# A convolution and mixture kernel with two layer norms: second norm statistics from ScalarE squares and a ones column, base sums and tail in the common order, modulation weights streamed, phases as integers

## The chip, the cores and the metric

The kernel runs on one core of one Trainium2 chip. The metric is the time of one execution in device microseconds. Inputs and output are bfloat16 and lie in the chip's memory. The core's engines work through queues of their own, in order: TensorE (PE in the profile, with PEld for its weight loads), VectorE (DVE), ScalarE (ACT), GpSimd (POOL), and SyncE (SP), which here only issues transfers.

## The reference

One sequence of 2048 tokens and 640 channels. A vector c gives six rows of modulation; x is normed and modulated, a gated long convolution over the tokens is added to it, and it is normed again. A router then picks 8 tokens, which pass through a gated feed-forward layer and are added back.

```python
mod = (silu(c) @ w_mod)                      # sa, ca, ga, sb, cb, gb
h = layernorm(x) * (1 + ca) + sa
kv = shift_conv(k, shift_k) * v              # 4 taps over the tokens
y = irfft(rfft(kv, 4096) * rfft(ssm_k, 4096))[:2048] + kv * ssm_D
x = x + ga * (h * y)
h = layernorm(x) * (1 + cb) + sb
r = h @ w_r                                  # 8 best tokens
y = (silu(h_sel @ w_gate) * (h_sel @ w_up)) @ w_down * sigmoid(r_sel)
x = x + gb * (h + scatter(y))
```

## The kernel before

The 640 channels are cut into 5 blocks of 128 (b = 0 to 4), the 2048 tokens into 16 tiles of 128 (m). All of x stays on chip as `xq` [128 x 16 x 640]. The Fourier transform of length 4096 is done as matmuls in two stages, with tables made on the chip: `RA` and `RAT` (`short_tables`, L202) and `FT` (`t_TAB`, L233), with `IT` its transposes.

Each block b goes through a chain of tasks. `C` makes kv: 16 matmuls with diagonals `dg` of the taps, then VectorE multiplies by v, and the result goes to memory (`kvd`) and comes back in another layout (`xA`, LXA). `G` and `X` do the first stage for filter and kv (8 matmul groups, evacuated into `A`), `B` the second (evacuated into `HX`), `P` the complex product on VectorE (L324 to L328). `BT` transforms back and writes `U` to memory as `Ud` from GpSimd's queue, `LU` loads it again as `uA`, `AT` finishes the transform, multiplies by h and adds to `xq` (L380, L382). The evacuations from PSUM go to ScalarE, or to VectorE where the task's name carries a star (`Evac`, L46).

Beside the blocks stand `LW` and `MOD` (six slices of the modulation weights, of 640 columns each, loaded into six places, and ten matmuls for each), `OG` and `COL` (products of modulation rows, router column `wcol` and its sum `wsum`), `LX` (x into `xq`; three of the six weight slices use `xq` before it), `Sx` (first norm statistics), `H` (h, 12 steps on VectorE), `S` (second norm statistics, bn_stats on 80 pieces of 128 columns, L390), `R` (transposes of `xq` and small matmuls with `wcol`, summed into `rsum`), and `WG`, `WD` (feed-forward weights).

What sets the order is the table `ORDER` (L34): a list of task names, each advanced by the number of steps behind the colon. The engines' queues, SP's and GpSimd's among them, hold instructions in just this order. Buffers rotate in pools, and an instruction waits by semaphore for what it reads and for its buffer.

Behind the table (from L586) follows the tail in the order of the code: `moments` and `rsqrt` of the second norm, the router scores `r_bf`, `norm` (16 tiles, six of them on ScalarE), the top 8 by rank on small tiles, `base` (four matmuls of 320 columns a tile add x and sb*gb in PSUM, ScalarE copies the sum over `xq`, L621), the selection of the 8 tokens by a one-hot matmul (L688), gate, up and down projection (L700, L731), `finish` (two VectorE operations for two tiles, stores of four tiles, L704), and the scatter with addition of 8 rows from GpSimd's queue (L739). Base sums stand in four places between selection, gate, up and down; four of the eight pairs of `finish` stand behind the down projection's `delta`.

Of the kernel before, what the change touches and what calls it, by code (L numbers as in the profile page):

```python
# [9 lines left out]
P = 128  # L10
# [16 lines left out]
MAGIC = 1.5 * float(2 ** 23)  # L27
TWO_PI = 2 * math.pi
# [31 lines left out]
def _kernel_body(ctx, tc, A_q, A_k, A_v, A_shift_k, A_ssm_k, A_ssm_D,  # L60
# [15 lines left out]
    front = ExitStack()  # L76
    psum = front.enter_context(tc.tile_pool(name="psum", bufs=4, space=bass.MemoryType.PSUM))
# [38 lines left out]
    scr = early[:, 2560:2560 + 2560].bitcast(F32)  # L116
# [18 lines left out]
    mc64 = const.tile([P, 2], F32, name="mc64")  # L135
    pc = const.tile([P, 1], F32, name="pc")
# [11 lines left out]
    ang = scr[:, 0:512].rearrange("p (s n) -> p s n", s=4)  # L148
    qn = scr[:, 512:1024].rearrange("p (s n) -> p s n", s=4)
    a4 = scr[:, 1024:1152]  # L150
# [6 lines left out]
    def t_START():  # L157
        load_kv(0)
        with nc.allow_non_contiguous_dma(reason="tiny transposed loads"):
            nc.scalar.dma_start(out=shk_bf[:], in_=A_shift_k.rearrange("(b p) j -> p b j", p=P))  # L160
            load_g(0, nc.scalar)
            nc.scalar.dma_start(out=cT_bf[:], in_=c.rearrange("o (t p) -> p (o t)", p=P))
            nc.scalar.dma_start(out=wr_c[:], in_=B_w_r.rearrange("(t p) -> p t", p=P))
        iota(pidx[:], [[0, 1]], cm=1)
        iota(arow[:], [[1, M], [0, 8]])
        iota(erow[:], [[0, M], [1, 8]])
        make_identity(nc, ident[:])
        for hf in range(2):
            iota(trig[:, hf, :].rearrange("p (a b) -> p a b", a=8), [[4, 8], [64, P]], base=32 * hf + 1)
        nc.gpsimd.memset(halfpi[:], math.pi / 2)  # L170
        nc.gpsimd.memset(Dt[:], 0.0)
        iota(irow[:], [[1, P]])
        nc.gpsimd.memset(onesb[:], 1.0)
# [28 lines left out]
    def short_tables(s0):  # L202
        src, col = (a4, 0) if s0 == 0 else (arf, 1)
        sl = slice(s0, s0 + 2)
        for s, sh in ((s0, 0.25), (s0 + 1, 0.5)):
            V.tensor_scalar(out=ang[:, s, :], in0=src, scalar1=mc64[:, col:col + 1], scalar2=sh, op0=ALU.mult,
                            op1=ALU.add)
        V.tensor_scalar(out=qn[:, sl], in0=ang[:, sl], scalar1=MAGIC, scalar2=None, op0=ALU.add)
        V.tensor_scalar(out=qn[:, sl], in0=qn[:, sl], scalar1=-MAGIC, scalar2=None, op0=ALU.add)
        V.tensor_tensor(out=ang[:, sl], in0=ang[:, sl], in1=qn[:, sl], op=ALU.subtract)  # L210
        nc.scalar.activation(out=trg[:, sl], in_=ang[:, sl], func=ACT.Sin, scale=TWO_PI)
        if s0 == 0:
            V.tensor_scalar(out=msk[:, 0, :], in0=ef, scalar1=ecol[:], scalar2=None, op0=ALU.is_equal)
            yield
# [3 lines left out]
        else:  # L218
            V.tensor_scalar(out=msk[:, 1, :], in0=msk[:, 0, :], scalar1=1.0 / 2048, scalar2=None, op0=ALU.mult)
            yield  # L220
# [12 lines left out]
    def t_TAB(hf):  # L233

        k0 = 8 * hf
        ph, qq, ab = trig[:, hf, :], trig[:, 2, :], trig[:, 3, :]
        fl = lambda s: FT[:, s, k0:k0 + 8, :].rearrange("p a b -> p (a b)")
        V.tensor_scalar(out=qq, in0=ph, scalar1=pc[:], scalar2=MAGIC, op0=ALU.mult, op1=ALU.add)
        V.tensor_scalar(out=qq, in0=qq, scalar1=-MAGIC, scalar2=None, op0=ALU.add)
        yield  # L240
        V.scalar_tensor_tensor(out=ph, in0=ph, scalar=pc[:], in1=qq, op0=ALU.mult, op1=ALU.subtract)
        nc.scalar.activation(out=fl(1), in_=ph, func=ACT.Sin, scale=TWO_PI)
        yield
        nc.scalar.activation(out=ab, in_=ph, func=ACT.Abs)
        nc.scalar.activation(out=fl(2), in_=ph, func=ACT.Sin, scale=-TWO_PI)
        nc.scalar.activation(out=fl(0), in_=ab, func=ACT.Sin, scale=-TWO_PI, bias=halfpi[:])
        yield
# [113 lines left out]
    rsum = small.tile([P, M, 2], F32, name="rsum")  # L361
    wcol = const.tile([P, NB, 2], BF, name="wcol")
# [22 lines left out]
    def t_S(b):  # L385
        if b == 0:
            h_["st2"] = small.tile([P, M, NB, 6], F32, name="st2", tag="st")
        st2 = h_["st2"]
        for m in range(M):
            V.bn_stats(out=st2[:, m, b, :], in_=xq[:, m, b * P:(b + 1) * P])  # L390
            if m % 4 == 3:
                yield

    def t_R(b):
# [6 lines left out]
        pr = ps_tile([P, M, 2])  # L401
# [11 lines left out]
    def t_LW():  # L413
        xf = xq[:].rearrange("p m d -> p (m d)")
        spare = trig[:].rearrange("p s n -> p (s n)").bitcast(BF)
# [32 lines left out]
    def t_COL():  # L448
# [13 lines left out]
        V.tensor_tensor(out=wcol[:, :, 1], in0=wp[:], in1=wcol[:, :, 0], op=ALU.subtract)  # L462
        red = small.tile([P, 2], F32, name="red")
# [89 lines left out]
    def t_WD():  # L553
# [4 lines left out]
        yield  # L558


    tasks = {}

    def once(f, b):
        f(b)
# [234 lines left out]
```

## Time and profile before

| what | us |
|---|---|
| median of 3 runs | 213.3 (212.53 to 213.63) |
| profiled execution, its own time | 213.28 |
| its span | 211.5 |
| mean granted TensorE clock | 0.879 of full |

The span is what the profile covers, from the first to the last instruction. A timeline row has start, duration, engine, line, operation, output<-input, the number of instructions and in brackets the idle time ahead of it with what ended it. A row of a group has the count, then the busy time in all and the mean ns of one, then the idle time ahead of it. A row of a transfer has its count, size, and the median time from issue to landing. In the chain that ended last a row has start, duration and what ran. Lines are those of the kernel as printed above.

### The profile page before, as it was taken

To read this page: it belongs to the slowest core of one execution; us is meant where nothing else is said; L and a number is where in the kernel's file an instruction comes from. 1 tells how busy PE (TensorE), PEld (TensorE's weight loads), DVE (VectorE), ACT (ScalarE), POOL (GpSimd) and SP (SyncE) were. 2 spreads that over 40 slices of the span, in tenths; PEclk is the share of its full clock that TensorE was granted. 3 is DMA by queue.
4 is the path that set the end of the run, shared out by engine and by line. 5 is a ranking of instruction groups with operands and counts; after the bars stand their busy time and mean duration, and the time that the engine had idled before them with its cause. 6 is when DMAs were issued, how large, how long until landed. Compare 5 with 4: busy or idle time off the path is not lost.

```text
span 211.5 us, 3596 instructions
## 1 busy us (share of the span) xinstructions
PE 152.4 (72%) x1388; PEld 107.4 (51%) x1398; DVE 167.1 (79%) x368; ACT 131.8 (62%) x144; POOL 27.5 (13%) x59
## 2 busy tenths in 40 slices
PE   0659849997849998999978998675831069979600
PEld 0224627675627664757666776565720038644300
DVE  7769844696858999999999999999999891092930
ACT  0568745678857998999999998563221562520700
POOL 8843100000011300002001102110041000000002
PEclk9999997999699999999999999999785557575955
DMA  7999999999999939004979955677939000015060
GB/s 135 174 219 257 247 362 362 256 274 287 324 241 285 196 100 198 3 0 149 361 207 353 337 165 214 205 223 215 387 103 335 2 0 3 3 64 187 15 233 2
DMA packets 67897, 40.64 MB, mean 192 GB/s; under 512 B 44768, under 2 KB 64680, under 8 KB 67880
## 3 DMA queue, kind: packets, MB, share of 16 engines
q1 hardware_dynamic: 62376, 34.62, 60.7%
q0 software_dynamic: 1472, 5.25, 6.4%
q10 hardware_dynamic: 4032, 0.53, 1.9%
q8 instruction: 11, 0.18, 0.4%
q14 instruction: 6, 0.05, 0.1%
HBM read 24.67 MB, written 10.50 MB: 166 GB/s over the span
## 4 chain that ended last, share of the span: by engine, by line
DVE 47%; issue 23%; PE 15%; DMA 6%; ACT 3%; POOL 2%; POOLq 1%; SPq 1%; DVEq 0%
DVE st L390 6%; DMA vT<-in_A_v_dram 5%; DVE t L380 4%; DVE T L324 3%; PE py L731 3%; ACT HX L57 3%; DVE kvT L290 3%; DVE h L539 3%; DVE h L535 3%; DVE h L541 3%; DVE st L524 3%; PE ps L288 2%; DVE HX L325 2%; DVE xn L709 2%; DVE xn L708 2%
## 5 line engine op out<-in xcount | busy, mean ns | idle before, releaser
L57 ACT CAST A<-ps 128x1024 bf16<-128x1024 f32 x36 | 36.1, 1080 | 7.9 <-PE ps L267 7.8
L57 ACT CAST HX<-ps 128x1024 bf16<-128x1024 f32 x38 | 37.0, 1119 | 1.8 <-PE ps L310 1.8
L288 PE MATMUL ps<-kT,dg 128*128 128x512 bf16 x77 | 20.2, 403 | 10.9 <-DMA kT<-in_A_k_dram 7.1
L306 PE MATMUL ps<-A,FT 128*128 128x512 bf16 x73 | 27.7, 379 | 0.3 <-ACT A L57 0.3
L57 ACT CAST U<-ps 128x1024 bf16<-128x1024 f32 x20 | 19.6, 1075 | 4.4 <-issue 3.7
L308 PE MATMUL ps<-A,FT 128*128 128x256 bf16 x80 | 21.8, 272 | 0.4
L310 PE MATMUL ps<-A,FT 128*128 128x256 bf16 x80 | 21.8, 273 | 0.0
L340 PE MATMUL ps<-IT,HX 128*128 128x256 bf16 x80 | 19.0, 280 | 3.6 <-DVE HX L327 2.6
L346 POOL DMA_DIRECT2D Ud<-U x10 | 5.7, 568 | 107.7 <-ACT U L57 107.7
L629 ACT CAST xq<-po 128x640 bf16<-128x640 f32 x16 | 10.6, 693 | 14.5 <-PE po L628 12.8
L342 PE MATMUL ps<-IT,HX 128*128 128x256 bf16 x80 | 18.8, 280 | 1.0 <-DVE HX L328 1.0
L288 PEld LDWEIGHTS <-dg 128*128 128x128 bf16 x80 | 8.0, 102 | 20.5 <-DVE dg L229 7.0
L57 ACT COPY xT<-ps 128x2048 bf16<-128x2048 bf16 x5 | 9.3, 1870 | 12.8 <-PE ps L397 12.8
L290 DVE TENSOR_TENSOR kvT<-ps,vT 128x1024 bf16<-128x1024 f32 x10 | 12.0, 1220 | 6.7 <-PE ps L288 3.9
L390 DVE BATCH_NORM_STATS2 st<-xq 128x6 f32<-128x128 bf16 x80 | 16.1, 278 | 0.0
L375 PE MATMUL ps<-RAT,uA 128*128 128x128 bf16 x160 | 11.3, 228 | 3.9 <-DVE t L380 3.4
L267 PE MATMUL ps<-RA,gA 128*128 128x256 bf16 x80 | 11.0, 273 | 3.8 <-DVE gA L274 3.8
L324 DVE TENSOR_TENSOR T<-HX 128x2048 bf16<-128x2048 bf16 x10 | 12.2, 1222 | 1.3 <-ACT HX L57 0.7
L524 DVE BATCH_NORM_STATS2 st<-xq 128x6 f32<-128x320 bf16 x32 | 12.8, 477 | 0.0
L375 PEld LDWEIGHTS <-uA 128*128 128x128 bf16 x160 | 10.3, 103 | 4.6 <-DMA uA<-Ud 2.4
L310 PEld LDWEIGHTS <-FT 128*128 128x128 bf16 x80 | 7.8, 98 | 9.4
L325 DVE TENSOR_TENSOR HX<-HX 128x2048 bf16<-128x2048 bf16 x10 | 12.2, 1225 | 0.4
(198 smaller groups left out, 314.3 us busy)
## 6 DMA issues: line engine op xcount, KB each, us to landing
Ud<-U POOLq DMA_DIRECT2D x10, 512.0 KB, 5.1
uA<-Ud SPq DMA_DIRECT2D x10, 512.0 KB, 5.4
kvd<-kvT SPq DMA_DIRECT2D x5, 512.0 KB, 3.4
xA<-kvd SPq DMA_DIRECT2D x5, 512.0 KB, 5.4
xq<-in_A_q_dram SPq DMA_DIRECT2D x4, 640.0 KB, 7.0
out_dram<-xn SPq DMA_DIRECT2D x4, 640.0 KB, 3.2
xq<-in_w_mod_dram SPq DMA_DIRECT2D x3, 800.0 KB, 11.5
wg<-in_B_w_gate_dram SPq DMA_DIRECT2D x1, 2160.0 KB, 12.3
```

The lines of the kernel that those rows point to most:

```text
L57: self.nc.scalar.copy(out=out, in_=in_)
L288: nc.tensor.matmul(ps[:, i, :], lhsT=diags[b][:, j, :], rhs=kT[:, n0 - j:n0 - j + 512], start=(j == 0), stop=(j == 3))
L290: V.tensor_tensor(out=kvT[:, 1024 * i2:1024 * i2 + 1024], in0=ps[:].rearrange("p a b -> p (a b)"), in1=vT[:, 1024 * i2:1024 * i2 + 1024], ...
L306: nc.tensor.matmul(ps[:, i, :], lhsT=FT[:, 0, k2, :], rhs=f(A[:, 2 * k2:2 * k2 + 2]), start=True, stop=False)
L308: nc.tensor.matmul(ps[:, i, 0:256], lhsT=FT[:, 1, k2, :], rhs=f(A[:, 2 * k2 + 1:2 * k2 + 2]), start=False, stop=False)
L310: nc.tensor.matmul(ps[:, i, 256:512], lhsT=FT[:, 2, k2, :], rhs=f(A[:, 2 * k2:2 * k2 + 1]), start=False, stop=True)
L324: V.tensor_tensor(out=T2[:], in0=X, in1=Hi, op=ALU.mult)
L340: nc.tensor.matmul(ps[:, i, :], lhsT=hx[:, k2, 0, 1, :], rhs=IT[:, k2, 1:3, :].rearrange("p a b -> p (a b)"), start=True, stop=False)
L342: nc.tensor.matmul(ps[:, i, :], lhsT=hx[:, k2, 1, 1, :], rhs=IT[:, k2, 0:2, :].rearrange("p a b -> p (a b)"), start=False, stop=True)
L375: nc.tensor.matmul(o, lhsT=uA[:, bb, cs * P:(cs + 1) * P], rhs=RAT[:, cs, :].rearrange("p (m e) -> p m e", e=8), start=(cs == 0), stop=(cs ...
L390: V.bn_stats(out=st2[:, m, b, :], in_=xq[:, m, b * P:(b + 1) * P])
L524: V.bn_stats(out=st1[:, m, hf, :], in_=xq[:, m, hf * 320:hf * 320 + 320])
```

## The change

The arithmetic is regrouped and the order table is written anew; nothing of the computation is left out.

- **Second norm.** Instead of bn_stats, ScalarE squares `xq` and sums (16 times 512 columns for blocks 0 to 3, then 11 times 128 for block 4), VectorE does five of block 4's; the sum of x comes from a third column of ones in `wcol`.
- **Base sums** are made from `ident` and 512-column pieces ahead of the statistics, into buffers of their own, and 128-column rests (`BL`) in two steps. Norm outputs go to the places of `FT` and `IT`, results and stores use `xq`.
- **The tail** is cut into tasks `T`, `N`, `F`, `BS`, `BL` and stands in the same order table and the same PSUM pool.
- **Modulation weights** are streamed through two places of `early`; `LX` is cut into four steps.
- **Phases** are integers: GpSimd multiplies, VectorE masks, ScalarE's sine takes scale and bias.

```diff
 def t_START():
     load_kv(0)
+    load_g(0)
...
-        load_g(0, nc.scalar)
...
+        G.tensor_scalar(out=trig[:, hf, :].bitcast(I32), in0=trig[:, hf, :], scalar1=pidx[:], scalar2=None,
+                        op0=ALU.mult)
...
 def t_TAB(hf):
-    V.tensor_scalar(out=qq, in0=ph, scalar1=pc[:], scalar2=MAGIC, op0=ALU.mult, op1=ALU.add)
-    V.tensor_scalar(out=qq, in0=qq, scalar1=-MAGIC, scalar2=None, op0=ALU.add)
-    yield
-    V.scalar_tensor_tensor(out=ph, in0=ph, scalar=pc[:], in1=qq, op0=ALU.mult, op1=ALU.subtract)
+    V.tensor_scalar(out=ph, in0=ph, scalar1=8191, scalar2=None, op0=ALU.bitwise_and)
...
+def squares(b0, nb, ms, on_act):
+    dst = ssq[:, 0 if b0 == 0 else 1, :]
+    n = nb * P
+    for m in ms:
+        src = xq[:, m, b0 * P:b0 * P + n]
+        if on_act:
+            nc.scalar.activation(out=junk()[:, 0:n], in_=src, func=ACT.Square, accum_out=dst[:, m:m + 1])
+        else:
+            V.scalar_tensor_tensor(out=junk()[:, 1024:1024 + n], in0=src, scalar=1.0, in1=src, op0=ALU.mult,
+                                   op1=ALU.mult, accum_out=dst[:, m:m + 1])
...
+def t_BS():
+    for j in range(8):
...
+        for i in range(2):
+            nc.tensor.matmul(ps[:, i, :], lhsT=ident[:], rhs=gbs[:, 0:512], start=True, stop=False)
+            nc.tensor.matmul(ps[:, i, :], lhsT=ident[:], rhs=xq[:, 2 * j + i, 0:512], start=False, stop=True)
+        evac(h_["base", j // 4][:, 2 * j % 8:2 * j % 8 + 2, 0:512], ps[:])
+        yield
...
 def t_LW():
-    homes = [early[:, 2560:5760], early[:, 5760:8960], xf[:, 0:3200], xf[:, 3200:6400], xf[:, 6400:9600],
-             spare[:, 0:3200]]
     for a in range(6):
-        wms[a] = homes[a].rearrange("p (t d) -> p t d", t=NB)
+        wms[a] = early[:, a % 2 * 3200:a % 2 * 3200 + 3200].rearrange("p (t d) -> p t d", t=NB)
...
+def t_F():
+    for j in range(8):
+        x2 = xq[:, 2 * j:2 * j + 2, :]
+        V.tensor_tensor(out=x2, in0=xn(2 * j, 2).rearrange("p (m d) -> p m d", m=2),
+                        in1=gbo[:, None, :].to_broadcast([P, 2, D]), op=ALU.mult)
+        V.tensor_tensor(out=x2, in0=x2, in1=h_["base", j // 4][:, 2 * (j % 4):2 * (j % 4) + 2, :], op=ALU.add)
+        if j % 2 == 1:
+            nc.sync.dma_start(out=out_d[:, 2 * j - 2:2 * j + 2, :], in_=xq[:, 2 * j - 2:2 * j + 2, :])
+        yield
...
+    V.tensor_scalar(out=mu[:], in0=rsum[:, :, 2], scalar1=1.0 / D, scalar2=None, op0=ALU.mult)
+    V.tensor_tensor(out=msq[:], in0=mu[:], in1=mu[:], op=ALU.mult)
+    V.scalar_tensor_tensor(out=tot[:], in0=ssq[:, 0, :], scalar=D * EPS, in1=ssq[:, 1, :], op0=ALU.add, op1=ALU.add)
+    V.scalar_tensor_tensor(out=vv[:], in0=tot[:], scalar=1.0 / D, in1=msq[:], op0=ALU.mult, op1=ALU.subtract)
```

The last line of the new table, with `BS*` and the like for an evacuation on VectorE:

```diff
+BS* S LU4 BS* R2 R3* WG S:2 AT4:2 SV TC R3 R4* SA:2 WD BS* BS R4 T BS:4 N* BL N:3 N*:2 N T F N T N* N N*:3 T
+F:2 N:3 T BL F:3 T:2 F:2 T:3
```

How the queues change shows at three places. First SP's queue near the start, before (kvd_196 and kvd_250 are blocks 0 and 1, early, xq and trig the places of the weight slices):

```order
L295 DMA kvd_196<-kvT 128x2048
L95 DMA_TRANSPOSE kT<-in_A_k_dram 128x2048
L96 DMA_TRANSPOSE vT<-in_A_v_dram 128x2048
L295 DMA kvd_250<-kvT 128x2048
L111 DMA xA<-kvd_196 128x16x128
L420 DMA early<-in_w_mod_dram 128x5x640 x2
L420 DMA xq<-in_w_mod_dram 128x5x640 x2
L295 DMA kvd_358<-kvT 128x2048
L106 DMA gA<-in_A_ssm_k_dram 128x16x128
```

and the same place in the change, where kvd_200 and kvd_263 are blocks 0 and 1:

```order
L297 DMA kvd_200<-kvT 128x2048
L106 DMA gA<-in_A_ssm_k_dram 128x16x128
L111 DMA xA<-kvd_200 128x16x128
L297 DMA kvd_263<-kvT 128x2048
L563 DMA xq<-in_A_q_dram 128x4x640
L111 DMA xA<-kvd_263 128x16x128
L95 DMA_TRANSPOSE kT<-in_A_k_dram 128x2048
L96 DMA_TRANSPOSE vT<-in_A_v_dram 128x2048
L563 DMA xq<-in_A_q_dram 128x4x640
L466 DMA early<-in_w_mod_dram 128x5x640
```

xA of block 0 has moved ahead of block 2's k and v; the first weight slice has moved behind both xA and half of x, and three more slices follow only after block 4's k and v.

Second, ScalarE's queue from the last transposes on, before (rs_1967 is the second norm's factor, po the base sums):

```order
L57 COPY xT<-ps 128x2048 x5
L616 ACTIVATE xn<-xq,nm_1986,rs_1967 128x640 x6
L629 CAST xq<-po 128x640 x4
L716 ACTIVATE gs<-pm 128x112
L629 CAST xq<-po 128x640 x4
L722 ACTIVATE sig_2328<-inf 8x1
L629 CAST xq<-po 128x640 x8
```

and in the change (FT and IT hold the norm outputs, rs_113 is the factor):

```order
L58 COPY xT<-ps 128x2048
L400 ACTIVATE junk,ssq<-xq 128x512 x16
L400 ACTIVATE junk,ssq<-xq 128x128 x11
L58 CAST base<-ps 128x2x512 x5
L58 CAST base<-ps 128x8x128
L621 ACTIVATE FT<-xq,nm_114,rs_113 128x640 x5
L621 ACTIVATE IT<-xq,nm_114,rs_113 128x640 x4
L58 CAST base<-ps 128x8x128
L725 ACTIVATE gs<-ps 128x112
L733 ACTIVATE sig_2295<-inf 8x1
```

27 squares have come in, nine norms instead of six, and seven base evacuations stand ahead of gs instead of ones on both sides of it.

Third, VectorE's queue from the middle of block 4's last update on, before:

```order
L380 TENSOR_TENSOR t<-ps,h 128x1024
L382 TENSOR_TENSOR xq<-xq,t 128x16x64
L407 TENSOR_TENSOR rsum<-rsum,ps 128x32
L390 BN_STATS st_1301<-xq 128x6 x24
L407 TENSOR_TENSOR rsum<-rsum,ps 128x32
L485 TENSOR_REDUCE bs<-st_1301 128x16
```

and in the change:

```order
L383 TENSOR_TENSOR t<-ps,h 128x1024
L385 TENSOR_TENSOR xq<-xq,t 128x16x64
L402 SCALAR_TENSOR_TENSOR junk,ssq<-xq 128x128 x5
L457 TENSOR_TENSOR rsum<-rsum,ps 128x48
L56 COPY xT<-ps 128x2048
L56 CAST base<-ps 128x2x512
L457 TENSOR_TENSOR rsum<-rsum,ps 128x48
L639 TENSOR_SCALAR mu<-rsum 128x16
```

The 24 statistics have become five squares, and one transpose copy and one base evacuation have come between the last update and the second norm's first operation.

More of the change, by code (lines that the diff above doesn't have):

```diff
@@ L27 @@
 MAGIC = 1.5 * float(2 ** 23)
+PI = 3.1415925
 TWO_PI = 2 * math.pi
@@ L621, in base @@
-    def base(ms):
-        for m in ms:
-            po = back.tile([P, 2, 512], F32, name="po", tag="o", bufs=2)
-            for hf in range(2):
-                cc = slice(hf * 320, hf * 320 + 320)
-                nc.tensor.matmul(po[:, hf, 0:320], lhsT=ident[:], rhs=gbs[:, cc], start=True, stop=False)
-                nc.tensor.matmul(po[:, hf, 0:320], lhsT=ident[:], rhs=xq[:, m, cc], start=False, stop=True)
-            nc.scalar.copy(out=xq[:, m, :].rearrange("p (h d) -> p h d", h=2), in_=po[:, :, 0:320])
@@ L678, in _kernel_body @@
-    V.tensor_copy(out=cinfo[:, 1:3], in_=cvp[:])
-    norm(rest[4:])
-    base(range(0, 4))
-    pin = pm_tile([NSEL, 3])
-    nc.tensor.matmul(pin[:, :], lhsT=ohC[:], rhs=cinfo[:], start=True, stop=True)
-    xsT = small.tile([P, NB, NSEL], BF, name="xsT")
-    pxs = pm_tile([P, NB, NSEL])
-    for b in range(NB):
-        for m in range(M):
-            nc.tensor.matmul(pxs[:, b, :], lhsT=xn[m // 8][:, m % 8, b * P:(b + 1) * P], rhs=onehot[:, m, :],
-                             start=(m == 0), stop=(m == M - 1))
```

417 lines of the change are left out of this document (217 added, 200 removed).

## The prediction

> **What bounds the kernel now.** I read the page's totals first, then busy time in four stretches, then the timelines of the engines and the chain that ended last. The first row is the page's; the others have start and end of a stretch, its length, the busy time of each engine (PE is TensorE, DVE VectorE, ACT ScalarE, POOL GpSimd), granted clock, DMA share and GB/s.
>
> ```profile
> PE 152.4 (72%) x1388; PEld 107.4 (51%) x1398; DVE 167.1 (79%) x368; ACT 131.8 (62%) x144; POOL 27.5 (13%) x59
> ...
> 0.00:62.00 62.00, 44.22 (x298) 28.83 (x302) 46.01 (x90) 39.08 (x42) 13.97 (x32) 0.94 1.06 262
> 62.00:134.40 72.40, 64.74 (x501) 46.48 (x507) 68.34 (x116) 65.65 (x71) 7.58 (x16) 1.00 0.69 194
> 134.40:156.30 21.90, 15.01 (x239) 13.78 (x239) 21.66 (x63) 9.30 (x6) 1.54 (x3) 0.92 0.74 246
> 188.60:195.60 7.00, 6.97 (x30) 3.37 (x30) 3.14 (x5) 0.00 (x0) 0.00 (x0) 0.57 0.54 190
> ```
>
> VectorE is the busiest engine and is idle 16.0 of the first 62 us, while the DMA share stands at 1. From 62 to 156.3 it works 90.0 of 94.3, with ScalarE close beside it until 134.4 and more than half free after. Call 134.4, the end of the last product P4, **T**, and 156.3, the end of the last add of the convolution's result into xq, **X**. From X on there is a serial tail of 55.2 us:
>
> ```profile
> 133.76 0.68 DVE L328 TENSOR_TENSOR HX<-HX,T 128x1024 bf16<-128x1024 bf16 x1
> ...
> 156.30 4.73 DVE L390 BATCH_NORM_STATS2 st<-xq 128x6 f32<-128x128 bf16 x24
> ...
> 161.07 0.36 DVE L485 TENSOR_REDUCE bs<-st 128x16 f32<-128x160 f32 x1
> ...
> 163.48 0.17 DVE L499 TENSOR_SCALAR n2v<-bw 128x16 f32<-128x16 f32 x1
> ...
> 166.72 0.23 DVE L605 TENSOR_SCALAR r_bf<-r,wsum 128x16 bf16<-128x16 f32 x1
> ...
> 172.14 2.23 DVE L618 TENSOR_SCALAR xn<-xq,rs,nm 128x640 bf16<-128x640 bf16 x6
> ...
> 177.67 0.20 DVE L694 TENSOR_TENSOR xsT<-xsf,mc 128x40 bf16<-128x40 f32 x1
> ...
> 188.63 6.88 PE L731 MATMUL py<-wd,hT 128*8 128x320 bf16 x28 [1.56 <-DVE hT L726]
> ...
> 196.36 0.80 DVE L708 TENSOR_TENSOR xn<-xn,modv 128x1280 bf16<-128x1280 bf16 x1
> ...
> 203.12 3.21 DMA out_dram<-xn
> ```
>
> So the tail reads: statistics 4.8 (to 161.07), moments and rsqrt 5.9 (to r_bf at 166.95), top-k, norms and selection 10.9 (to xsT at 177.87), gate and up with base sums between them 10.8, down projection 6.9, and 16.0 after it, in which four output pairs (6.8, 1.69 each) and the last store (landed at 206.33) still stand ahead of the scatter.
>
> **Part 1, up to T: VectorE's work.** Each half of the phase tables loses three passes and gets one integer mask. A dozen small START and short-table passes go to GpSimd or vanish. Twelve of 80 statistics ahead of T go. Twelve evacuations instead of 7 stand ahead of T, and one more update (t, then xq).
>
> ```profile
> L238 DVE TENSOR_SCALAR trig<-trig,pc 128x1024 f32<-128x1024 f32 x2 | 1.5, 744 | 0.0
> ...
> L241 DVE SCALAR_TENSOR_TENSOR trig<-trig,pc 128x1024 f32<-128x1024 f32 x2 | 2.7, 1339 | 0.0
> ...
> L55 DVE CAST A<-ps 128x1024 bf16<-128x1024 f32 x4 | 4.8, 1218 | 4.2 <-PE ps L267 4.2
> ...
> L380 DVE TENSOR_TENSOR t<-ps,h 128x1024 bf16<-128x1024 f32 x10 | 12.1, 1214 | 0.0
> ...
> L382 DVE TENSOR_TENSOR xq<-xq,t 128x1024 bf16<-128x1024 bf16 x10 | 6.9, 692 | 0.3
> ```
>
> The three passes are two like L238 and L241: 2.8 a half, 5.6. An integer mask is not in the trace; between 0.74 and 1.34 I take L238's: two cost 1.5, so 4.1 are saved. Small passes: about 3 (estimate, 12 at 0.15 to 0.4). Statistics: 12 at 0.2 (24 took 4.73), 2.4. Against this 5 x 1.22 = 6.1 and 1.9 for the update. Net some 1.4 saved.
>
> **Part 1: VectorE's idle time.** The waits that matter, and their prices:
>
> ```profile
> 30.48 2.56 PE L432 MATMUL ps<-early 128*128 128x320 bf16 x10 [2.99 <-DMA early<-in_w_mod_dram]
> ...
> 33.93 2.36 DVE L55 CAST A<-ps 128x1024 bf16<-128x1024 f32 x2 [4.18 <-PE ps L267]
> ...
> 2.12 2.11 POOL L155 IOTA trig<- 128x1024 f32 x2
> ...
> 5.75 4.22 POOL L229 TENSOR_SCALAR dg<-ident,shk_f 128x128 bf16<-128x128 bf16 x4 [0.79 <-DVE shk_f L226]
> ...
> L198 POOL TENSOR_SCALAR tri<-irow,pidx 128x128 bf16<-128x128 f32 x1 | 0.6, 627 | 0.0
> ...
> L193 POOL TENSOR_SCALAR mC<-pidx 128x1 f32<-128x1 f32 x1 | 0.2, 183 | 0.0
> ...
> kvd<-kvT SPq DMA_DIRECT2D x5, 512.0 KB, 3.4
> xA<-kvd SPq DMA_DIRECT2D x5, 512.0 KB, 5.4
> ...
> xq<-in_w_mod_dram SPq DMA_DIRECT2D x3, 800.0 KB, 11.5
> ...
> early<-in_w_mod_dram SPq DMA_DIRECT2D x2, 800.0 KB, 8.2
> ```
>
> Now stage X0 stands on TensorE behind the first modulation matmul, which waits for its weights; the new order puts it ahead. kvd0 can leave near 15.5 (below), land in 3.4, xA0 in another 5.4: X0 near 25 instead of 33. The 4.2 us wait goes, and with it about 2 behind it. **What is late next**: the first quarter of q, whose statistics move up to this place (I charge 2), and GpSimd, which now makes the phases. Its 1024-wide multiply is not in the trace. From 0.18 for one column and 0.63 for 128, that is 3.5 ns a column, it is 3.7; its ends are the 1.05 of an iota as wide and 8 x 1.06 = 8.4, from four dg that took 4.22 beside a busy VectorE. I take 3.7, nearest to the plain fp32 row. With the first iota done near 5 the second phase table is ready near 13.5; its mask (0.75) stands on VectorE ahead of the second kvT (1.2), hence 15.5; I charge 1. So 3 us less idle; ends: 6 less (neither charge) to 6 more (multiplies at 8.4, twice 4.7, less the 3). T = 134.4 - 1.4 - 3 = 130.0.
>
> The Trainium skill, GPSIMD Engine Reference, Performance versus the Vector engine, speaks against this move: GpSimd is about half as fast as VectorE at elementwise work and needs about 2.6 cycles an element at 1.2 GHz. That would be an estimated 2.2 us a multiply, and T 1 us earlier; the 3.5 ns a column of the trace is dearer than the page's figure.
>
> **Part 2, T to X.** Now 21.9, all VectorE: 7 updates (13.3) and 44 statistics (8.7). After: 6 updates (11.4), two xT and two base evacuations (4.9), small ones (0.4): 16.7. But uA4's path becomes late. Its last evacuations now end 3.1 after T, at 137.45; then write, load, matmul:
>
> ```profile
> 135.52 1.93 ACT L57 CAST U<-ps 128x1024 bf16<-128x1024 f32 x2 [2.64 <-issue]
> ...
> Ud<-U POOLq DMA_DIRECT2D x10, 512.0 KB, 5.1
> uA<-Ud SPq DMA_DIRECT2D x10, 512.0 KB, 5.4
> ```
>
> 3.1 + 5.1 + 5.4, about 1.2 for two issues and 0.9 for sixteen matmuls are 15.7, where VectorE arrives at 12.9. Two updates (3.8) follow: X = 130.0 + 19.5 = 149.5.
>
> **Part 3, the tail.** ScalarE squares 16 rows of 512 columns from the last AT3 update on (some 12 before X), then 11 of 128 after X.
>
> ```profile
> L211 ACT ACTIVATE early<-early 128x256 bf16<-128x256 f32 x2 | 0.8, 416 | 1.2 <-DVE early L210 1.1
> ...
> 166.07 4.98 ACT L616 ACTIVATE xn<-xq,nm,rs 128x640 bf16<-128x640 bf16 x6 [6.55 <-DVE nm L600]
> ...
> 118.81 7.43 ACT L57 CAST HX<-ps 128x1024 bf16<-128x1024 f32 x8
> ...
> L688 PE MATMUL pm<-onehot,xn 128*128 128x8 bf16 x80 | 2.2, 166 | 0.0
> ...
> L700 PE MATMUL pm<-xsT,wg 128*128 128x8 bf16 x70 | 2.0, 168 | 0.5 <-DVE xsT L694 0.5
> ```
>
> A square with a sum is not in the trace. A wide one lies between 0.42 (256 columns) and 0.93 (1024, from 7.43 for 8); I take 0.75, nearest to the 0.83 of 640. A narrow one: 0.15 to 0.42, I take 0.35. The wide ones then end at X, the narrow at X+4; at the upper ends X+3 and X+8. Beside them block 4's row sums need transposes, a copy behind five VectorE squares, and 16 small matmuls behind eight base matmuls at half clock: about X+5.4. The chain starts at X+5.5, now 4.8: no gain. It has 18 small operations; now 17 lie between 163.48 and 166.72: 3.7 to r_bf, at X+9.2.
>
> The Trainium skill, ScalarE: Activation LUTs, What ACT_TABLE_LOAD costs, gives 186 ns and 0.833 a column, 93 for each pointer operand, 93 overlapped. That is 0.81 for the 640-column norm, and the 0.83 here agrees; a wide square would be an estimated 0.52 and end 3.7 earlier. The page has no price for the sum, and X+5.4 would still hold.
>
> Selection needs all 16 normalized tiles. ScalarE first has six base evacuations (0.93 each), until about X+10.5, then nine norms (0.83): X+18; 80 matmuls add 2.2. VectorE has three norms fewer than now in this place (7.4 falls to 6.3), but three output pairs (5.1), and some 2 of waiting for a transpose queued on TensorE behind cold base matmuls: 13.5, xsT at X+22.7. Here the change loses 2.6. But gate and up run back to back, 2.0 each, with three pairs beside them: 5.2 to the down projection instead of 10.8. It takes 6.9 again. Behind it stand only delta (0.9) and the scatter, 5.2 from its release to the end (206.33 to 211.5): 6.1 instead of 16.0, since all eight pairs are ahead. 5.5 + 3.7 + 13.5 + 5.2 + 6.9 + 6.1 = 40.9, against 55.2.
>
> 149.5 + 40.9 = 190.4 of span. The profiled execution took 213.28 for its 211.5, so 1.8 lie around it, and the median of three runs is 213.3. Forecast **192.2 us**.
>
> **Rivals.**
> 1. GpSimd contended: multiplies at 8.4 delay the front by 6 to 9: 198 to 202. The 4.22 of dg speaks for it; against it, VectorE has less to do there than now.
> 2. ScalarE overfull: the chain starts at X+8 to X+10 and the norms follow: 195 to 198.
> 3. A warm TensorE: 6.9 x 0.57 is 3.9 at full clock, so 189; with the front's lower end 184. The Trainium skill, TensorE: Matmul & The Clock Gate, Part 1, gives full clock after about 3.4 us of sustained work; the mean of 0.57 over seven dense microseconds here does not bear that out.
> 4. **Slower: the streaming.** Six weight slices share two buffers. Slice a waits for matmul a-2; SP, in order, holds k, v and g loads behind it, and TensorE everything behind a modulation matmul. Five landings laid bare at 8.2 to 11.5 are 41 and more: 233. It decides from 4.2 us exposed per slice, 21 in all. Against it: counting VectorE's work ahead of each place in the new order and 12 of idle, the second and third go out near 49 for use near 58 to 62, and the last is needed only ahead of h, near 88.
> 5. It doesn't do what it says: the statistics change engine and X to chain start stays as long. That I expect (5.5 against 4.8); the gain rests on the order of pairs, gate and up, which the queues fix.
>
> **How the numbers follow.** Forecast (187 to 196) 0.55; rival 1 0.13; rival 2 0.12; rival 3 0.11; rival 4 in part (203 to 212) 0.03 and whole 0.06. The range 184 to 202 takes in the ends of T and of the squares. A measurement of this kernel tells 0.5% (1.1 us) from no change: faster 0.91, same 0.02, slower 0.07.
>
> **What would show it.** X0 near 25 and no TensorE wait over 3 us on a modulation slice: streaming is hidden. T near 130, X near 150, narrow squares done near X+4, gate and up without base sums between them, nothing but delta and the scatter behind py. Wrong: T at 134 or later means that the new order brought nothing, and a delta that waits for pairs that the end is no shorter.

## The result, and the profile after

| | before | after |
|---|---|---|
| median | 212.9 us (212.53 to 213.63, 4 runs) | 189.3 us (188.03 to 190.83, 4 runs) |
| profiled execution, its span | 213.28, 211.5 | 188.81, 187.0 |

The ratio is 0.889 (95% interval 0.882 to 0.897): 11% faster, where 192.2 us was forecast. The first view is the busy time by stretch, cut at the same events as before: T, X, r_bf, xsT, start and end of py.

```profile
0.00:62.00 62.00, 49.82 (x340) 32.05 (x341) 50.95 (x82) 44.67 (x47) 24.98 (x48) 0.97 1.02 239
62.00:130.20 68.20, 62.31 (x533) 46.26 (x531) 63.44 (x106) 58.20 (x63) 4.44 (x10) 0.97 0.82 237
130.20:146.20 16.00, 11.89 (x190) 10.00 (x187) 15.76 (x20) 11.93 (x26) 6.00 (x12) 1.00 0.80 264
146.20:157.70 11.50, 9.38 (x60) 4.96 (x60) 7.24 (x32) 11.03 (x36) 0.83 (x3) 0.85 0.72 238
157.70:169.70 12.00, 3.94 (x88) 2.99 (x89) 10.96 (x35) 9.57 (x12) 0.00 (x0) 0.59 0.11 40
169.70:175.10 5.40, 4.97 (x144) 4.14 (x143) 5.06 (x10) 1.36 (x3) 0.00 (x0) 0.50 0.46 157
175.10:181.70 6.60, 6.54 (x28) 3.13 (x28) 3.19 (x6) 0.00 (x0) 0.00 (x0) 0.60 0.59 202
```

The columns are those of the same view of the kernel before. Up to T VectorE works as long as before: 50.95 + 63.44 = 114.4, against 46.01 + 68.34 = 114.35. Its idle time fell from 20.05 to 15.8. From T to X it works 15.76 of 16.0, where it worked 21.66 of 21.9. The timelines of the engines, at the events:

```profile
129.56 0.68 DVE L330 TENSOR_TENSOR HX<-HX,T 128x1024 bf16<-128x1024 bf16 x1
...
145.47 0.69 DVE L385 TENSOR_TENSOR xq<-xq,t 128x1024 bf16<-128x1024 bf16 x1
...
151.53 0.18 DVE L640 TENSOR_TENSOR msq<-mu 128x16 f32<-128x16 f32 x1
154.55 0.17 DVE L641 SCALAR_TENSOR_TENSOR tot<-ssq 128x16 f32<-128x16 f32 x1 [2.85 <-ACT junk L400]
...
157.42 0.23 DVE L648 TENSOR_SCALAR r_bf<-r,wsum 128x16 bf16<-128x16 f32 x1
...
169.49 0.20 DVE L710 TENSOR_TENSOR xsT<-xsf,mc 128x40 bf16<-128x40 f32 x1
...
175.09 6.54 PE L738 MATMUL ps<-wd,hT 128*8 128x320 bf16 x28 [0.43 <-DVE hT L729]
...
181.68 0.87 DVE L743 SCALAR_TENSOR_TENSOR delta<-ps,sig,modv 8x640 bf16<-8x640 f32 x1 [3.34 <-PE ps L738]
182.88 1.51 POOL L747 DMA_INDIRECT out_dram<-delta,idx  x1 [27.15 <-DVE delta L743]
```

The mean is ready at 151.5, and VectorE waits 2.85 for ScalarE's squares: a new wait at the head of the serial chain. Gate and up have no base sums between them, and nothing but delta and the scatter stands behind py. The tail from X to the end is 40.8, against 55.2.

### The profile page after: what moved, and what is told of

Its sections match the earlier page's. It is cut to its first block, busy times and chain, and to the rows that moved or that the text cites. A ratio compares the mean times of both kernels' runs of the same rounds, so it can differ in the third digit from the quotient of the medians.

```text
span 187.0 us, 3521 instructions
## 1 busy us (share of the span) xinstructions
PE 148.8 (80%) x1374; PEld 103.5 (55%) x1374; DVE 157.4 (84%) x283; ACT 136.8 (73%) x184; POOL 37.8 (20%) x74
## 4 chain that ended last, share of the span: by engine, by line
DVE 32%; ACT 20%; PE 20%; DMA 12%; issue 6%; POOL 6%; POOLq 1%; SPq 0%; DVEq 0%
ACT junk L400 8%; DVE t L383 5%; PE ps L290 5%; ACT HX L58 3%; DMA early<-in_w_mod_dram 3%; DMA xq<-in_A_q_dram 3%; POOL trig L178 3%; DVE kvT L292 3%; DVE h L586 3%; PE ps L478 3%; DVE h L584 3%; DVE h L580 3%; ACT base L58 3%; DMA uA<-Ud 3%; DVE T L326 3%
## 5 line engine op out<-in xcount | busy, mean ns | idle before, releaser
L58 ACT CAST A<-ps 128x1024 bf16<-128x1024 f32 x34 | 33.4, 1059 | 6.9 <-PE ps L269 6.9
L58 ACT CAST HX<-ps 128x1024 bf16<-128x1024 f32 x36 | 35.4, 1060 | 3.6 <-PE ps L312 3.4
L308 PE MATMUL ps<-A,FT 128*128 128x512 bf16 x80 | 30.5, 382 | 1.4 <-ACT HX L58 0.6
L310 PE MATMUL ps<-A,FT 128*128 128x256 bf16 x80 | 21.9, 274 | 0.0
L312 PE MATMUL ps<-A,FT 128*128 128x256 bf16 x80 | 21.9, 273 | 0.0
L58 ACT CAST U<-ps 128x1024 bf16<-128x1024 f32 x19 | 18.5, 1087 | 2.9 <-issue 1.5
L342 PE MATMUL ps<-IT,HX 128*128 128x256 bf16 x80 | 18.1, 272 | 0.3 <-DVE t L383 0.3
L344 PE MATMUL ps<-IT,HX 128*128 128x256 bf16 x80 | 18.1, 272 | 0.0
L400 ACT ACTIVATE junk<-xq 128x512 bf16<-128x512 bf16 (+1 forms) x27 | 13.5, 499 | 2.6 <-DVE xq L385 1.7
L478 PE MATMUL ps<-early 128*128 128x320 bf16 x60 | 10.3, 328 | 2.8 <-DVE early L473 2.0
L269 PE MATMUL ps<-RA,xA 128*128 128x256 bf16 x80 | 12.1, 298 | 0.1
L383 DVE TENSOR_TENSOR t<-ps,h 128x1024 bf16<-128x1024 f32 x10 | 12.2, 1216 | 0.0
L233 POOL TENSOR_SCALAR dg<-ident,shk_f 128x128 bf16<-128x128 bf16 x16 | 11.7, 746 | 2.1 <-PE ps L290 2.1
```

The costliest lines, as they stand in the source:

```text
L58: self.nc.scalar.copy(out=out, in_=in_)
L269: nc.tensor.matmul(ps[:, bb // 2, :, (bb % 2) * 8:(bb % 2) * 8 + 8], lhsT=src[:, 4 * g4 + bb, :], rhs=RA[:].rearrange("p k c e -> p (k c) ...
L308: nc.tensor.matmul(ps[:, i, :], lhsT=FT[:, 0, k2, :], rhs=f(A[:, 2 * k2:2 * k2 + 2]), start=True, stop=False)
L310: nc.tensor.matmul(ps[:, i, 0:256], lhsT=FT[:, 1, k2, :], rhs=f(A[:, 2 * k2 + 1:2 * k2 + 2]), start=False, stop=False)
L312: nc.tensor.matmul(ps[:, i, 256:512], lhsT=FT[:, 2, k2, :], rhs=f(A[:, 2 * k2:2 * k2 + 1]), start=False, stop=True)
L342: nc.tensor.matmul(ps[:, i, :], lhsT=hx[:, k2, 0, 1, :], rhs=IT[:, k2, 1:3, :].rearrange("p a b -> p (a b)"), start=True, stop=False)
```

## Experiments

The theory: T to X is VectorE's own work, so the statistics count whole; the order of the pairs saves what stood behind py; the front gained because X0 no longer waits for a modulation product; the squares on ScalarE cost some 3 at the chain's start. Ratios are to the kernel before on the same chip, with 95% intervals. The yardstick is the changed kernel run again:

> The changed kernel as it is, on the same chip as the next three: the yardstick for differences of a few us, since two profiles with the same front showed T at 130.2 and at 132.2. Expected 188 to 191.

189.0 us, ratio 0.895 (0.890 to 0.900), T at 131.0. In six other kernels whose code up to T is the change's, profiles have T between 129.1 and 132.2, so one profile tells T to about 1.5. The intervals of the next two kernels are some 0.02 to either side, which is 4 us.

### Statistics back on VectorE

```diff
-AT2:2 BT4:2 LU3 AT3 R1 AT3 S R1 R2*
-BS* S LU4 BS* R2 R3* WG S:2 AT4:2 SV TC R3 R4* SA:2 WD BS* BS R4 T
+AT2:2 BT4:2 LU3 AT3 R1 AT3 S0:4 R1 R2* S1:4
+BS* LU4 BS* R2 R3* WG S2:4 S3:4 AT4:2 TC R3 S4:4 R4* WD BS* BS R4 T
```

`S` is bn_stats as in the kernel before, and `moments` takes the place of the new sums.

> The changed kernel with only the second norm's statistics put back to bn_stats on VectorE: 64 pieces between the updates of block 3 and of block 4, 16 behind the last update and ahead of the transposes' copy; ScalarE's 27 squares and VectorE's five are gone. Theory A (VectorE's work sets T to X, so statistics taken off it are worth their whole time): X moves from 146.2 by 64 x 0.197 = 12.6 to about 158.8, r_bf by about 13 with the longer moments, of which some 1.5 come back because ScalarE's base sums are done ahead of the norms: 188.8 + 11 = about 200. Theory B (the gain is all in the order of the tail, and the squares cost at the chain's start what they save before X): within 2 us of 189.

Ratio 0.945 (0.926 to 0.963), 199.7 us: some 10.6 more than the changed kernel (0.050 of 212). Last add, first operation of the moments, and r_bf on VectorE's timeline:

```profile
157.17 0.69 DVE L385 TENSOR_TENSOR xq<-xq,t 128x1024 bf16<-128x1024 bf16 x1
...
163.37 0.36 DVE L536 TENSOR_REDUCE bs<-st 128x16 f32<-128x160 f32 x1
...
168.25 0.23 DVE L649 TENSOR_SCALAR r_bf<-r,wsum 128x16 bf16<-128x16 f32 x1
```

T is at 129.6, so T to X is 28.3 instead of 15.9: the 64 pieces add 12.4, nearly the 12.6 expected as their whole time. The moments start 5.5 after X instead of 8.4, and r_bf is 10.8 later; from there it is 28.2 to the end instead of 29.6, of which 1.0 is a shorter py. Theory A holds.

### Last four pairs behind delta

```diff
-F:2 N:3 T BL F:3 T:2 F:2 T:3
+F:2 N:3 T BL F T:4 F:4 T
```

> The changed kernel with only the last four output pairs moved behind delta, as they stood before. Theory A (what stands between delta and the scatter is laid bare whole): four pairs of 1.65 are 6.6, then a store that lands 3.2 after its issue, ahead of the scatter: about 199, py end to span end about 15.5 instead of 5.4. Theory B (the pairs only fill time that VectorE waits anyway, and the scatter does not wait for them): under 2 us.

Ratio 0.940 (0.922 to 0.959), 200.3 us, some 9.6 more. From the chain that ended last, and GpSimd's timeline:

```profile
189.78 0.84 DVE xq L631
190.64 3.21 DMA out_dram<-xq
...
194.91 1.51 POOL L747 DMA_INDIRECT out_dram<-delta,idx  x1 [37.24 <-issue]
```

delta ended at 184.2; the scatter started 10.7 later, behind four pairs and a store, and from py's end to the end of the span it is 15.7 (15.5 expected). Theory A holds.

### The pairs alone, and with the base sums ahead, in the kernel before

```diff
-    finish(range(2, 4))
+    finish(range(2, 8))
     delta = ...
-    finish(range(4, 8))
```

and in the second kernel also `base(range(8, 16))` ahead of py instead of 8 to 10 there and 10 to 16 behind it.

> The kernel before with one part of the change alone: the last four output pairs moved ahead of delta. Theory A (the order of the pairs works only together with the early base sums): pair 4 runs beside py, but pairs 5 to 7 wait for base sums that stand behind py on TensorE; the last store lands about 1 earlier than at 206.3: 0.5 to 2 less than before. Theory B (the order of the pairs by itself brings what it costs to undo it in the changed kernel): 7 to 10 less.

> The kernel before with two parts of the change: the last four pairs ahead of delta, and the last six base sums ahead of py on TensorE instead of behind it. Theory A (pairs and base sums go together): py starts some 4 later for 24 more matmuls and ScalarE's copies, but the pairs end beside it and nothing but delta and the scatter stands behind: 3 to 5 less than before, against 1.8 less for the pairs alone. Theory B (what matters is that the base sums leave the tail altogether): what the pairs gain the later py takes back, 0 to 2 less than before.

Ratios 0.990 (0.986 to 0.994) and 0.993 (0.989 to 0.997): 2.1 and 1.5 us less than before. py of the first and its last store; then py of the second, and on its VectorE the first operation after xsT and delta:

```profile
189.10 3.97 PE L731 MATMUL py<-wd,hT 128*8 128x320 bf16 x28 [1.57 <-DVE hT L726]
...
199.27 3.22 DMA out_dram<-xn
```

```profile
193.27 3.97 PE L731 MATMUL py<-wd,hT 128*8 128x320 bf16 x28
...
186.78 0.14 DVE L723 TENSOR_SCALAR sig<-sig 8x1 f32<-8x1 f32 x1 [6.52 <-ACT sig L722]
...
200.06 0.87 DVE L735 SCALAR_TENSOR_TENSOR delta<-py,sig,modv 8x640 bf16<-8x640 f32 x1
```

In the first, delta has to wait for the pairs, and one of these 0.4 for a base sum behind py; the store ends at 202.5 and the scatter begins at 203.5. In the second, py starts 4.2 later, but that is not what holds the end: py is over at 197.2, and delta starts at 200.1, straight behind the pairs and without a wait. In both kernels VectorE idles 6.5 us while gate and up run, and six pairs, 10 us, then stand between hT and delta. For the second kernel the time is theory B's, though not for the reason that B gives.

So undoing the pair order costs 9.6, but doing it alone, or with base sums still in the tail, brings 2. In the change three pairs run ahead of xsT and three more beside gate and up, and they can because their base sums are made by then. That this is what makes the difference is read from the traces; no run moved the base sums alone. Nor do all of them stand ahead of the statistics: of the eight sums of 512 columns VectorE copies two at 138.9 and one at 149.8, and ScalarE copies five from 154.4 on, behind its squares and ahead of its norms.

### The first modulation product ahead of X0

```diff
-... C0 LG1 G0*:3 G0 RAT DIAG1 LXA0 C1:2 IT:2 G1* IT* X0 X0* X0 X0*
+... C0 LG1 LW G0*:3 G0 RAT DIAG1 LXA0 C1:2 IT:2 G1* IT* RAT MOD X0 X0* X0 X0*
```

> The changed kernel with the first modulation slice loaded and multiplied ahead of stage X0, as it stood before; streaming and all else stay. Theory A (X0 ahead of the modulation product is what the front gained): X0 starts 3 to 5 us later than 23.5, T goes from 130.2 to about 133, time about 192. Theory B (VectorE's 11 us of idle time in the front absorb it): T within 1 us, time 188 to 190.

Ratio 0.906 (0.887 to 0.925), T at 130.7. The time does not separate the theories; T is within the changed kernel's 129.1 to 132.2, though X0 starts at 28.5 instead of 23.5. Here the weights are asked for so early that they have landed; the product waits 3.5 for a copy on VectorE instead. The next kernel asks for them behind xA0 (`... LXA0 C1:2 LW IT:2 ...`):

> As the kernel with the first modulation slice ahead of stage X0, but its weights are asked for only behind xA0 in SP's queue, so that the product waits for its transfer and holds X0 as it did before. Theory A (the exposed wait was what the front lost): MOD waits some 5 to 7 for its weights, X0 starts near 31 to 33 as before, T goes from about 131 to 134 to 135, time 192 to 193. Theory B (VectorE meets its later waits earlier and nothing is lost): X0 as late, but T within 1.5 of the changed kernel's 130.2 and 131.0.

Ratio 0.915 (0.908 to 0.921): some 4 us more than the changed kernel, outside both intervals. TensorE, then VectorE's last product:

```profile
30.23 2.54 PE L478 MATMUL ps<-early 128*128 128x320 bf16 x10 [4.35 <-DMA early<-in_w_mod_dram]
32.56 2.60 PE L269 MATMUL ps<-RA,xA 128*128 128x256 bf16 x16
```

```profile
136.84 0.68 DVE L330 TENSOR_TENSOR HX<-HX,T 128x1024 bf16<-128x1024 bf16 x1
```

X0 starts at 32.6, as it did before (32.8), and T moves to 137.5, which is 5 to 8 later than the changed kernel's 129.1 to 132.2. This one execution took 1.3 us more than its median, and its first filter stage was slow ahead of the edit (3.59 instead of 1.92, see below), so the 4 us of the times are the better measure. The transfer laid bare ahead of X0 costs these 4 us, as theory A says; X0 5 us late behind a product whose weights lie ready moves T by less than the scatter. Whether it is the transfer itself or what it delays in SP's queue was not separated.

### Phases in floating point again

```diff
-        V.tensor_scalar(out=ph, in0=ph, scalar1=8191, scalar2=None, op0=ALU.bitwise_and)
+        V.tensor_scalar(out=qq, in0=ph, scalar1=pc8[:], scalar2=MAGIC, op0=ALU.mult, op1=ALU.add)
+        V.tensor_scalar(out=qq, in0=qq, scalar1=-MAGIC, scalar2=None, op0=ALU.add)
+        V.scalar_tensor_tensor(out=ph, in0=ph, scalar=pc8[:], in1=qq, op0=ALU.mult, op1=ALU.subtract)
```

> The changed kernel with the long tables' phases in floating point again: GpSimd's two multiplies go, VectorE makes three passes a half instead of one mask. Theory A (VectorE's wait of 1.42 for GpSimd gives back most of the 3.8 of work that was saved): second kvT ends about 1 us later, time about 190. Theory B (the work saved counts whole): 193. Theory C (GpSimd was the brake): 187 to 188.

Ratio 0.907 (0.892 to 0.922), 192.1 us, T at 133.5: some 2.6 more, nearer to B, though the interval reaches A and no change at all. The first filter stage on TensorE, in this kernel and in the changed one:

```profile
15.88 3.48 PE L272 MATMUL ps<-RA,gA 128*128 128x256 bf16 x16 [4.99 <-DVE gA L279]
```

```profile
14.56 1.92 PE L269 MATMUL ps<-RA,gA 128*128 128x256 bf16 x16 [3.07 <-DVE gA L276]
```

VectorE reaches it 1.3 later, which is the phases' own doing. That the sixteen matmuls take 3.48 instead of 1.92 is not: in the changed kernel's second run they took 3.46 too, behind a wait of only 2.14. Of nine executions with the change's code up to there, three took 1.92, one 2.43 and five 3.46 to 3.59, behind waits of 2.1 to 3.7 in no order. T lies at 129.1 to 130.2 in the three and at 130.5 to 132.2 in the others that keep the change's code up to T. Against those, the 133.5 here is 1.3 to 3.0 later.

### A warm TensorE

```diff
+    def warm(n):
+        pw = ps_tile([P, 512])
+        for _ in range(n):
+            nc.tensor.matmul(pw[:, :], lhsT=ident[:], rhs=gbs[:, 0:512], start=True, stop=True)
```

`warm(5)`, `warm(7)` and `warm(4)` stand in the three waits of the selection.

> The changed kernel with 16 matmuls of 512 columns added whose results nobody reads, in three places of the tail where TensorE waits for VectorE (5 behind the scores' transpose, 7 behind the candidates' products, 4 behind the one-hot product). Theory A (idling in the selection is what lowers the granted clock): the clock stays above 0.9 until py, py falls from 6.5 towards 3.9 and gate and up from 3.9 towards 3. Then the last pair's store, at present landing 1.1 ahead of delta's end, holds the scatter, so the time falls by 1 to 2 only. Theory B (gate, up and the selection's 8-column matmuls do not hold the clock): the clock is near 0.5 again in gate and up, py stays at 5.5 to 6.5 and the time within 1 of the kernel without them.

Ratio 0.896 (0.889 to 0.902): no change. Stretches of this kernel, then the same of the changed kernel's second run (the third number from the end is the granted clock):

```profile
165.00:169.70 4.70, 3.37 (x85) 2.50 (x84) 4.62 (x10) 2.96 (x4) 0.00 (x0) 0.85 0.14 48
169.70:175.00 5.30, 5.30 (x145) 4.20 (x142) 4.86 (x9) 1.36 (x3) 0.00 (x0) 0.50 0.60 207
```

```profile
165.00:169.70 4.70, 2.54 (x76) 2.22 (x76) 4.63 (x10) 3.06 (x4) 0.00 (x0) 0.50 0.12 41
169.70:175.10 5.40, 5.40 (x148) 4.30 (x146) 4.92 (x10) 1.36 (x3) 0.00 (x0) 0.50 0.60 206
```

The clock rose from 0.50 to 0.85 in the one-hot stage, and fell to 0.50 again in gate and up; py took 5.31, against 5.27 without. Theory B holds, and rival 3 can't be had this way.

### The chain's start, and the tail's order

The first kernel moves six narrow squares to VectorE (`SV` in steps of 5, 2 and 4 rows, `SA` one of 5) and the row sums ahead of two base sums:

```diff
-R4* SA:2 WD BS* BS R4 T
+R4* SA WD SV R4 SV BS:2 T
```

> The changed kernel with six of block 4's eleven ScalarE squares moved to VectorE (two behind the last transposes' copy, four behind its row sums), the row sums ahead of two base sums, and the evacuation of one base sum moved from VectorE to ScalarE. Theory A (the squares on ScalarE hold the chain's start, and ScalarE's queue of base sums and norms holds the selection): VectorE's sum of squares starts near X+5.9 instead of X+8.4, r_bf near X+8.8 instead of X+11.4, but xsT only about 1.3 earlier, since ScalarE still has seven base sums and nine norms ahead of it: about 1.3 less. Theory B (r_bf alone holds the selection): all 2.5 arrive, 2.5 less. Theory C (the row sums hold the start, not the squares): no gain.

```profile
150.77 0.17 DVE L643 SCALAR_TENSOR_TENSOR tot<-ssq 128x16 f32<-128x16 f32 x1 [0.47 <-ACT junk L400]
...
156.87 0.28 DVE L659 CAST rT<-ps 16x128 f32<-16x128 bf16 x1 [1.73 <-PE ps L657]
...
165.27 0.19 PE L707 MATMUL ps<-onehot,IT 128*128 128x8 bf16 x1 [0.62 <-ACT IT L623]
```

and the last of these in the changed kernel:

```profile
167.32 0.19 PE L705 MATMUL ps<-onehot,IT 128*128 128x8 bf16 x1 [0.62 <-ACT IT L621]
```

X is 145.0 here: the chain starts at X+5.8 instead of X+8.4 and r_bf ends at X+8.9, as theory A says, but xsT is only 0.9 earlier (X+22.7 instead of X+23.5). VectorE has a new wait, since the scores' transpose stands on TensorE behind base sums that run there without a gap until 156.6. What holds xsT is ScalarE, in both kernels: the one-hot products wait 0.62 for its last norm, which ends at X+20.2 instead of X+21.1, the same 0.9. That is theory A's reason: base sums and norms fill ScalarE's queue. Ratio 0.893 (0.888 to 0.897), not separable from the changed kernel. The next two also change the order behind T:

```diff
-BS:4 N* BL N:3 N*:2 N T F N T N* N N*:3 T F:2 N:3 T BL F:3 T:2 F:2 T:3
+BS:2 N* BL N:3 N*:2 T BS:2 N:2 N* N:2 F T BL N*:3 T N*:2 F:2 T F:3 T:2 F:2 T:3
```

```diff
-BS:2 N* BL N:3 N*:2 T BS:2 N:2 N* N:2 F T BL N*:3 T N*:2 F:2 T F:3 T:2 F:2 T:3
+BS BL N* N:3 N*:2 T BS:3 N:2 N* N N* F T BL N*:3 T N*:2 F:2 T F:2 T:2 F:3 T:3
```

> The changed kernel with the squares split as in the kernel before this, and the tail's order changed: the scores' transpose ahead of the last two base sums, nine instead of seven norms on VectorE's and seven on ScalarE's side, the second set of 128-column rests behind the candidates' products instead of ahead of gate. Theory A (ScalarE's queue of base sums and norms, and the transpose stuck behind base sums, held the selection): xsT near X+21.3 instead of X+23.5, py start near X+26 instead of X+28.9, end near X+38 instead of X+40.7: 2 to 3 less than the changed kernel, ratio to before near 0.882. Theory B (VectorE's work in the tail is the bound by itself): within 1 of it.

> The kernel before this, with three moves in the tail: two pairs instead of three ahead of hT, the scores' transpose ahead of three base sums instead of two, and one more norm on VectorE. Theory A (hT stood 1.57 behind pairs that now fill VectorE's queue, the transpose 0.95 behind base sums, and the last norms on ScalarE 1.1 in the one-hot products): py starts near X+25.5 instead of X+27.6, the last pair is stored 1 earlier, 1 to 2 less than the kernel before this, ratio to before near 0.875. Theory B (the pairs' total on VectorE and the last store set the end, whatever stands ahead of hT): within 0.5 of it.

Ratios 0.882 (0.876 to 0.888) and 0.880 (0.875 to 0.884), both 187.0 us. py of the first, then py, last store and scatter of the second:

```profile
174.09 6.70 PE L740 MATMUL ps<-wd,hT 128*8 128x320 bf16 x28 [1.57 <-DVE hT L731]
```

```profile
171.93 5.46 PE L740 MATMUL ps<-wd,hT 128*8 128x320 bf16 x28 [0.43 <-DVE hT L731]
...
176.74 3.21 DMA out_dram<-xq
...
181.01 1.51 POOL L749 DMA_INDIRECT out_dram<-delta,idx  x1 [27.65 <-issue]
```

The first has the ratio that theory A expected. In it (X at 146.5), xsT came at X+22.1 instead of the expected X+21.3, and hT then waited behind three pairs. In the second (X at 146.4), py starts at X+25.5 as foretold, 2 earlier than in the first; delta is done at 178.3, but the scatter begins at 181.0, after the last store landed at 180.0. The median did not move, as theory B says; the intervals alone would leave room for 1 us less. What sets the end in this execution is VectorE's eight pairs and the store behind them. By the ratios both kernels are some 3 us faster than the changed kernel (0.013 and 0.015 of 212), by the medians 2.

## Why the prediction was right, and where it was wrong

| step | forecast | measured |
|---|---|---|
| T | 130.0 | 130.2 |
| T to X | 19.5 | 15.9 |
| X to chain start | 5.5 | 8.4 |
| to r_bf | 3.7 | 3.1 |
| to xsT | 13.5 | 12.0 |
| to py | 5.2 | 5.4 |
| py | 6.9 | 6.5 |
| to the end | 6.1 | 5.4 |

**T** was right by luck: two errors cancel. No VectorE work was saved (forecast 1.4), and 4.2 instead of 3 of idle time went. Of the missing work, the masks have 0.3 (0.88 each, not 0.75) and the small passes some 0.6 (2.4 saved, not 3); the rest is spread. That the transfer in front of the modulation product delayed X0, and that this cost time, is borne out by the kernel that lays it bare again (4 us). Streaming was hidden, as forecast; rival 4 did not come: TensorE waited 0.4 in all for a slice. GpSimd's multiply took 3.0 each, under the 3.7 taken, and VectorE waited 1.42 for the second; rival 1 did not come.

**T to X was the step that failed**: "uA4's path becomes late", 15.7 after T. The evacuations ended at T+3.2 as forecast; write, load and issues then took 7.5 for the first half of uA4 and 9.3 for the second, not 11.7 for both. ScalarE's last evacuations, GpSimd's last write, the two last writes from issue to landing, then TensorE:

```profile
131.46 1.93 ACT L58 CAST U<-ps 128x1024 bf16<-128x1024 f32 x2 [1.53 <-issue]
...
133.68 0.53 POOL L348 DMA_DIRECT2D Ud<-U  x1 [2.93 <-ACT U L58]
...
Ud<-U POOLq DMA_DIRECT2D x2, 512.0 KB, 3.6
...
140.92 1.07 PE L378 MATMUL ps<-RAT,uA 128*128 128x128 bf16 x16 [0.21 <-DMA uA<-Ud]
142.68 1.07 PE L378 MATMUL ps<-RAT,uA 128*128 128x128 bf16 x16 [0.69 <-DMA uA<-Ud]
```

The 5.1 that I took for a write was the median of all ten; the two last ones landed in 3.6 (their median). The sum also let both updates wait for the second half, while the first needs only the first. VectorE never waited for uA4, and X followed its own work, estimated at 16.7 and measured at 15.8. It was close: the second half's matmuls ended at 143.75, and VectorE took them up at 144.21. So the statistics were worth more than the sum gave them; undoing them cost 10.6. Rival 5 came true from X on (8.4 to the chain's start, against 4.8 before), but T to X did get shorter.

**The chain's start** was mis-sized on ScalarE. The squares by form, with the read of the sum that each takes behind it:

```profile
L400 ACT ACTIVATE junk<-xq 128x512 bf16<-128x512 bf16 x16 | 10.1, 630 | 2.2 <-DVE xq L385 1.7
...
L400 ACT ACTIVATION_READ_ACCUMULATOR junk<-xq 128x1 f32 x27 | 5.0, 186 | 0.0
...
L400 ACT ACTIVATE junk<-xq 128x128 bf16<-128x128 bf16 x11 | 3.4, 309 | 0.3
```

Wide ones follow each other every 0.755 (0.75 was taken), narrow ones every 0.435 (0.35 was taken, with 0.42 as the upper end). The squares run from the last AT3 update, 137.7 (137.5 by the sum), whatever X does. As X came 3.3 ahead of forecast, they ended at X+8.4, not X+4; from the start of the span the chain began at 154.6, against 155.0. So the misses of T to X and of the chain's start are for the most part one: what X gained, the chain lost to ScalarE. The split moved the start by 2.6. The row sums were ready 5.2 after X (5.4 forecast).

**The selection** had one charge too many: the transpose did not wait behind base sums, since the chain came late. It did as soon as the start moved forward, by 1.73. And the sum took VectorE's work as its length, while ScalarE set it: its base sums ended at X+13.8 instead of X+10.5, its last norm at X+21.1 instead of X+18, and the one-hot products waited for that norm. This is rival 2 as it was described, the late start and the norms that follow, without its time, since X was early. **Gate and up, py, and the end** were within 0.7 of the forecast; rival 3 did not come, py had a clock of 0.60.

The forecast was 2.9 us above the median, and its span 3.4 above the profiled one (190.4 against 187.0). T to X (3.6), the selection (1.5) and r_bf, py and the end (1.7 together) were too long, the chain's start 2.9 too short, T and gate and up 0.2 each. That the sum came so near is in part this cancelling.

## What to carry over

Where an engine is busy through a stage, work taken off it counts whole; a path expected to come late in its place needs its transfers' times from a stretch like it, not the median of the whole kernel. An operation order that costs 9.6 us to undo in one kernel may bring only 2 in another: here the pairs ahead of delta pay where most of them can run before the down projection, and for that they need their base sums early. When a serial chain is started earlier, look again at what its next links are queued behind, on every engine.

## What the runs showed of the hardware

- The sum behind a ScalarE square costs an instruction of its own, 186 ns, more than half of a 128-column square (309 ns). As the two overlap in part, it lengthens each square by some 125 ns (630 to 755, 309 to 435).
- The granted clock of the same work differs from execution to execution. In the changed kernel py took 6.54 in one and 5.27 in the other, behind the same wait of 0.4. It took 6.88 at a mean clock of 0.57 in the kernel before, and 3.97 in the variant of it with the pairs ahead, behind the same wait of 1.6. The 0.57 of the kernel before is the mean of a step: 0.50 until 194, full from 195 on. The Trainium skill, TensorE: Matmul & The Clock Gate, Part 1, says that the window over which activity is judged runs freely, so that the cold time varies from run to run; this agrees.
- In gate and up the clock did not rise: 140 matmuls of 8 columns ran 3.9 us at 0.50, and where matmuls had been added ahead the clock fell to 0.50 from 0.85. In the changed kernel they end a stretch of 7.3 us, from 167.4 to 174.7, in which TensorE had work without a gap at 0.50. The Trainium skill, on the same page and in the same part, gives some 3.4 us of sustained work for full clock; here that did not suffice. Whether the few columns are the reason was not separated.
- The 256-column integer mask of the short tables took 1.18 on VectorE while GpSimd made the phases, and 0.29 later, in the changed kernel:

```profile
5.20 1.18 DVE L216 TENSOR_SCALAR early<-early 128x256 int32<-128x256 int32 x1
...
19.38 0.29 DVE L216 TENSOR_SCALAR early<-early 128x256 int32<-128x256 int32 x1
```

In the kernel with phases in floating point GpSimd does not multiply, and the mask still took 1.03, while GpSimd wrote a 1024-wide iota (4.39 to 5.43):

```profile
4.54 1.03 DVE L218 TENSOR_SCALAR early<-early 128x256 int32<-128x256 int32 x1
```

So the multiply is not needed for it. Such rows are work that the sum did not have; that GpSimd's work beside them is the cause is likely, and no run separates it.
